# A feature-map attention and a Mish feed-forward in one core: other loads at the start, bias by columns, nine filler products, and a new order of all steps

## The chip, the cores and the metric

The kernel runs on one core of a Trainium2 chip. The metric is the device time of one execution in microseconds (us). A core has five engines that run side by side and wait for each other by semaphores: PE (matrix products), DVE and POOL (vector work), ACT (functions of one operand), SP (here it only issues DMAs). The instructions of one engine run in the order in which they are written.

## The reference

```python
x = A_x                                    # 1 x 2048 x 448, bf16
xn = _layernorm(x)
# A: 16 heads of 28 columns
q, k, v = split(xn @ wqkv)
phi_q = concat(softmax(q @ w_phi), softmax(-q @ w_phi))
phi_k = concat(softmax(k @ w_phi), softmax(-k @ w_phi))
kv = phi_k^T @ v ;  z = sum of phi_k over the rows
o = (phi_q @ kv) / (phi_q @ z + 1e-6)
# B: 448 -> 1792 -> 448
h = xn @ w1 + b1
act = h * tanh(softplus(h))                # Mish
out = x + o @ wo + act @ w2
```

## The kernel before, in words

**Tiles.** The 2048 rows are 16 tiles (t) of 128 rows, handled as 8 pairs (u). A pair is normalised (statistics on DVE, L472 and L473, 1/sqrt on ACT or POOL, the scaling on DVE, ACT or POOL) and transposed to `xnT`: pairs 3 and 1 by PE in two parts (`xT_part`, L530, with an evacuation in `evac`, L565 on ACT or L567 on DVE), the other six by a DMA that transposes (L572, on SP's queue). For the key and query features the kernel first multiplies the weights with `w_phi`: the key weights are transposed on PE (`w_tr`, L612), the query weights come transposed by four DMAs (`load_qT`, L292; `double_qT`, L296, copies a part of them), and `w_mm` (L641) multiplies both with a block-diagonal `Wbd` that POOL fills (`w_bd`, L595).

**Products.** Every value (v), key (k), query (q) and first feed-forward (f) step is a pair of accumulations over 448 rows. 448 is three and a half times 128, so a step has a part F, six products over 128 rows, and a part H, two products over 64 rows each that run beside each other in the two halves of the array. All of them are recorded in `pair_part` (L440), which takes a pair of PSUM banks when the first part of a step is issued and gives it back after the second; there are four such pairs. The step's result leaves the banks by an exponential on ACT (keys L678, queries L740), by a copy on ACT or DVE (values, L565 and L567) or by Mish on ACT (L774). The first F parts of v3, k3, v1 and k1 wait separately for the two halves of `xnT` (`SPLIT`).

**The rest.** The exponentials are normalised by DVE (sum and reciprocal) and POOL (the product, L690 for keys, L755 for queries). The eight `kv` steps (L707) add up keys times values, `kvz` makes the matrix that the `nd` steps (L800) multiply with the query features, which SP's queue has transposed by then (`q_turn`, L763). The outputs are transposed by DMA (L817). Per tile the output is a sum of `g` (L883, 14 products) and `wo` (L899); DVE adds x (L848) and SP stores.

**The order.** `ORDER` is a string with the names of all steps; `run_order` calls them in that order, and each step appends its instructions to its engines' queues. `v3Fd` is part F of the values of pair 3 with DVE as evacuating engine, `lx1s` the load of pair 1's rows on SP, `st7d` the statistics of tile 7 on DVE, `xm7d` the scaling of tile 7 on DVE (`xm7p` on POOL), `xa3a` the first part of the transposition of pair 3 with ACT as evacuating engine, `z10` ten filler products without use (L384), `wtk0b` and `wmk0b` the two halves of the key weights. The string is read together with the waits that `Program.resolve` derives from who writes and reads what.

**What the change touches.** `load_kv_tail` (L286) brings the last 64 rows of key and value weights in one DMA of 896 columns, `load_v_tail` (L289) the value columns a second time into the upper 64 partitions, since H products of the second tile read there; the upper half of the key tail is set to zero by DVE (`p_wz`, L348). `load_b1` (L309) brings the bias as 14 rows of 128, and `bias_T` (L768) turns them by a product on PE and a copy on DVE.

Of the kernel before, what the change touches and what calls it, by code (L numbers as in the profile page):

```python
# [151 lines left out]
ORDER = """  # L152
pm pw lx3s pk pz lkms lkts lvms lvts lpa table pi lx1s lqT0 lx2s st6d rt6a st7d z10 rt7a lqT1 lx4s lqT2 lqT3 xm6d lx0s
pv wtk0b lx6s xm7d xa3a wtk1b bd wmk0b xb3a st3d wmk1a st2d v3Fd st5d rt3p rt2a xm2d v3Ha xm3d lbs k3F st4d xa1a k3H
xb1d v1Fa qd wmq1a rs2p st11d xn2d wmq0a st10d k1F b1 k1H st13d rs5p xn5p v1Ha q1H q3H st9d st12d q1F q3F xt2m q2F k2F
st8d st0d k2H rs4p v2Hd st1d l1m1s xt5m xn4d rs6p rs0p l1m2s xt4m q2H xn6p st15d st14d v2Fd rs7p xt6m k5F xn0p q5F pp
q5H xn7d k5H v4Ha k4H v4Fd qn6p xt7m l1m0s k4F qn4p q6F k6F v5Ha q6H qn7p qn2p k7H xt0m l1ts e7 k6H v5Fd kn3.0 k7F q7F
v6Fa q7H kn1.1 kn4.1 kn1.0 q0H qn13p f1.0H v6Ha q0F kn2.1 f1.0F f0.1F f0.5F v0Fd f0.1H f0.5H f1.2H kn3.1 v0Hd f1.2F
f1.5F f1.4H f1.5H k0H kn7.0 kn6.1 kn2.0 v7Hd kn7.1 ep f1.4F k0F v7Fd qn14p q4F f1.3F q4H kn5.1 e6 f0.2H f1.3H f0.0H
kn0.1 f0.2F f0.0F e2 f0.3F e4 kn6.0 kv7 e14 kn5.0 kn0.0 kv1 kv3 f0.9H f0.3H f0.9F los f1.1F kn4.0 f0.13F f0.10F f0.13H  # L160
f1.1H qn11p qn12p kv5 kv0 kv6 kv2 kv4 f0.12H f0.6H f0.10H f0.6F qn3p kvz qn9p f0.12F qn5p f1.6F e3 qn1p f1.6H qn8p
f0.4H f1.10H f0.7H qn0p f1.10F f0.4F nd7 wob e5 qn15p f0.7F nd4 f1.9F f0.11F f1.12F f0.11H f1.12H f1.8H f1.9H f1.8F
f1.7F f1.13F qn10p l2s f1.13H e15 f1.11H f0.8H f1.7H e9 f0.8F nd2 f1.11F nd6 e8 g5 nd3 nd5 e11 e10 e12 g8 ot3m ot1m
ot2m nd8 g3 g9 nd9 ot4m nd11 g2 wo2F wo3F e13 wo4H e1 wo1H wo2H wo3H wo1F g4 nd10 wo4F nd13 ot5m sto2 nd14 g7 g6 nd15
e0 g13 sto4 sto1 nd0 nd1 wo5F g14 ot7m ot0m g10 nd12 g12 g0 wo7F g1 ot6m wo0H wo7H wo6H wo5H wo6F stt14 sto3 g11 wo0F
sto0 sto5 sto6 g15 stt15
"""
# [7 lines left out]
def _kernel(es, nc, A_x, A_wqkv, A_w_phi, A_wo, B_w1, B_b1, B_w2, out):  # L175
    def sb(name, shape, dtype):
        return es.enter_context(nc.sbuf_tensor(name, shape, dtype))
# [588 lines left out]
    def bias_T():  # L766
        b = take1()
        pe(lambda e: e.transpose(bank16(b)[:, 0:FC], b1_rows[0:FC, :], ident[0:FC, 0:FC]), [("b1r",), ("ident",)],  # L768
           [pb(b)], "b1")
# [275 lines left out]
```

## Time and profile before

| | |
|---|---|
| median of 3 runs | 151.9 us (151.89 to 152.0) |
| the profiled execution | 151.9 us, of which its span is 150.4 us |
| busy time DVE, ACT, POOL | 90.3 us (60%), 71.4 us (47%), 70.4 us (47%) |
| DMA | 16.97 MB in 39480 packets, mean 113 GB/s |
| shares of the chain that ended last | PE 89%, SP's queue 5%, DMA 2%, DVE 1% |

The span runs from the first instruction to the last; 1.5 us of the execution lie outside it. A start in the rows below is counted from the start of the span. The busy time of PE is that of pipelined products whose ends overlap, so how fast PE runs is read from the distance between starts, not from the duration of one.

### The profile page before, as it was taken

The page shows a single profiled execution, that of the slowest core. Times are in us where ns is not written, and L with a number is a line of the kernel's source. Part 1 is how long each engine was busy: PE and PEld are TensorE (multiplying, and loading weights), DVE is VectorE, ACT ScalarE, POOL GpSimd, SP SyncE. Part 2 cuts the span into 40 slices and gives each one's busy share as a digit, 9 for nine tenths or more (in the row PEclk, how much of TensorE's full clock was granted, in tenths as well). Part 3 has the DMA queues.
Part 4 walks back from the last instruction along what each step waited for, and adds up shares of the span by engine and source line. Part 5 has one row for each costly group of instructions (what it writes and reads, how often), then busy time and mean ns, then how long its engine had stood idle before and what let it go on. Part 6 is the DMA issues. An engine that isn't in the chain of part 4 may idle for free.

```text
span 150.4 us, 2592 instructions
## 1 busy us (share of the span) xinstructions
PE 146.1 (97%) x1051; PEld 72.3 (48%) x1051; DVE 90.3 (60%) x180; ACT 71.4 (47%) x85; POOL 70.4 (47%) x77
## 2 busy tenths in 40 slices
PE   7899999999999999999999999999999999999992
PEld 2554444444443535454354445555455555554451
DVE  0997996899999899947986004514049351200641
ACT  3688998989986979546681974000000000000000
POOL 7522799399999999998999100000000000000000
PEclk9999999999999999999999999999999999999999
DMA  5997696796830009401479994530905933030206
GB/s 131 271 234 215 127 251 114 142 226 40 174 70 0 0 0 126 162 0 29 80 145 355 155 197 89 101 65 9 188 3 39 256 86 61 0 65 0 92 0 214
DMA packets 39480, 16.97 MB, mean 113 GB/s; under 512 B 33452, under 2 KB 38700, under 8 KB 39468
## 3 DMA queue, kind: packets, MB, share of 16 engines
q1 hardware_dynamic: 38860, 16.68, 51.6%
q10 hardware_dynamic: 608, 0.12, 0.4%
q8 instruction: 8, 0.13, 0.3%
q14 instruction: 4, 0.03, 0.1%
HBM read 6.97 MB, written 1.84 MB: 59 GB/s over the span
## 4 chain that ended last, share of the span: by engine, by line
PE 89%; SPq 5%; DMA 2%; DVE 1%; issue 0%
PE PS L440 49%; PE PS L883 28%; PE PS L899 7%; PE PS L800 2%; DMA WqT<-in_A_wqkv_dram 2%; SPq L292 2%; PE PS L707 2%; SPq L271 1%; SPq L274 1%; PE PS L641 1%; DVE x_all L848 0%; SPq L286 0%; SPq L289 0%; DVE WqT L296 0%; DVE x_all L869 0%
## 5 line engine op out<-in xcount | busy, mean ns | idle before, releaser
L440 PE MATMUL PS<-xnT,W 128*128 128x512 bf16 (+1 forms) x224 | 45.5, 379 | 0.0
L883 PE MATMUL PS<-W,actT 128*128 128x448 bf16 (+1 forms) x224 | 44.0, 351 | 0.0
L774 ACT ACTIVATE actT<-PS,b1T 128x1024 bf16<-128x1024 f32 x28 | 30.1, 1113 | 13.3 <-PE PS L440 13.1
L883 PEld LDWEIGHTS PS<-W,actT 128*128 128x128 bf16 x224 | 21.4, 98 | 18.8
L440 PEld LDWEIGHTS PS<-xnT,W 128*128 128x128 bf16 (+1 forms) x224 | 17.6, 97 | 24.4 <-issue 5.4
L755 POOL TENSOR_TENSOR EqS<-EqS,rSk 128x896 bf16<-128x896 bf16 x16 | 26.7, 1694 | 3.0 <-DVE rSk L753 3.0
L690 POOL TENSOR_TENSOR actT<-actT,rSk 128x896 bf16<-128x896 bf16 x16 | 26.6, 1693 | 0.0
L848 DVE TENSOR_TENSOR x_all<-PS,x_all 128x448 bf16<-128x448 f32 (+1 forms) x16 | 9.5, 617 | 20.8 <-PE PS L899 14.4
L805 DVE RECIPROCAL rden<-PS 128x16 f32<-128x16 f32 x16 | 4.0, 250 | 24.2 <-PE PS L800 24.2
L751 DVE TENSOR_REDUCE Sk<-EqS 128x32 f32<-128x896 bf16 x16 | 16.7, 1042 | 0.0
L686 DVE TENSOR_REDUCE Sk<-actT 128x32 f32<-128x896 bf16 x16 | 16.5, 1033 | 0.0
L740 ACT ACTIVATE EqS<-PS 128x896 bf16<-128x896 f32 x16 | 13.8, 943 | 2.6 <-PE PS L440 2.6
L678 ACT ACTIVATE actT<-PS 128x896 bf16<-128x896 f32 x16 | 13.7, 941 | 0.2 <-PE PS L440 0.2
L440 PE MATMUL PS<-Wkv,xnT 128*128 128x448 bf16 (+1 forms) x64 | 13.2, 353 | 0.0
L440 PE MATMUL PS<-Wpk,xnT 128*128 128x448 bf16 (+1 forms) x64 | 13.0, 353 | 0.0
L440 PE MATMUL PS<-Wpq,xnT 128*128 128x448 bf16 (+1 forms) x64 | 12.5, 353 | 0.0
L472 DVE BATCH_NORM_STATS2 stats<-x_all 128x6 f32<-128x448 bf16 x16 | 9.7, 608 | 2.6 <-DMA x_all<-in_A_x_dram 2.6
L807 DVE TENSOR_TENSOR xn<-PS,rden 128x448 bf16<-128x448 f32 x16 | 10.0, 625 | 0.6
L440 PEld LDWEIGHTS PS<-Wpq,xnT 128*128 128x128 bf16 (+1 forms) x64 | 5.2, 97 | 6.2 <-issue 1.9
L440 PEld LDWEIGHTS PS<-Wkv,xnT 128*128 128x128 bf16 (+1 forms) x64 | 5.0, 97 | 6.0 <-issue 1.9
L440 PEld LDWEIGHTS PS<-Wpk,xnT 128*128 128x128 bf16 (+1 forms) x64 | 5.3, 97 | 5.2 <-issue 0.6
L567 DVE CAST v_all<-PS 128x896 bf16<-128x896 f32 x5 | 5.4, 1079 | 2.3 <-PE PS L440 2.3
(80 smaller groups left out, 108.7 us busy)
## 6 DMA issues: line engine op xcount, KB each, us to landing
W<-in_B_w_dram SPq DMA_DIRECT2D x1, 1568.0 KB, 9.0
out_dram<-x_all SPq DMA_DIRECT2D x7, 224.0 KB, 2.3
W<-in_B_w_dram SPq DMA_DIRECT2D x3, 448.0 KB, 3.9
x_all<-in_A_x_dram SPq DMA_DIRECT2D x4, 224.0 KB, 3.5
x_all<-in_A_x_dram SPq DMA_DIRECT2D x2, 448.0 KB, 4.2
Wkv<-in_A_wqkv_dram SPq DMA_DIRECT2D x2, 336.0 KB, 4.1
Wo<-in_A_wo_dram SPq DMA_DIRECT2D x2, 336.0 KB, 4.0
W<-in_B_w_dram SPq DMA_DIRECT2D x2, 224.0 KB, 4.7
```

The lines of the kernel that those rows point to most:

```text
L440: ins = e.matmul(o, lhs(c, k), rhs(c, k), start=first and c in (0, 3), stop=not first and c in (2, 3))
L472: op("DVE", lambda e: e.bn_stats(stats[:, t, :], x_all[:, t, :]), r=[("x", t)], w=[("st", t)], tag=f"bn{t}")
L678: op("ACT", lambda e, s=s: e.activation(E_of(u)[:, s, :, :], two(b, D), ACT.Exp, scale=1.0 if s == 0 else -1.0), r=[pb(b), pb(b + 1)], w=[ ...
L686: op("DVE", lambda e: e.tensor_reduce(Sk[u][:, s, :], Eh(), AX.X, ALU.add), r=[("E", u, s)], w=[("Sk", u, s)], tag=f"Sk{u}.{s}")
L690: op("POOL", lambda e: e.tensor_tensor(Eh(), Eh(), ap_on(rSk[u][:, s, 0:1], [[1, 2 * H], [0, DH]]), ALU.mult), r=[("E", u, s), ("rSk", u, ...
L740: op("ACT", lambda e, s=s: e.activation(EqS[:, k:k + 2, :, s * QP:(s + 1) * QP], two(b, D).rearrange("p i (h n) -> p i h n", n=QP), ACT.Ex ...
L751: op("DVE", lambda e: e.tensor_reduce(ap_on(Sk[u][:, i, 0:1], [[4, 2 * G], [1, 4]]), E, AX.X, ALU.add), r=both, w=[("Sk", u, i)], tag=f"Sq ...
L755: op(eng, lambda e: e.tensor_tensor(E, E, ap_on(rSk[u][:, i, 0:1], [[4, 2 * G], [1, 4], [0, DH]]), ALU.mult), r=both + [("rSk", u, i)], w= ...
L774: op("ACT", lambda e: e.activation(actT[:, fc, q * 1024:(q + 1) * 1024], bank(b, 2), ACT.Mish, bias=b1T[:, fc:fc + 1]), r=[("b1T",), pb(b) ...
L807: op("DVE", lambda e: e.tensor_tensor(o_sb[u % NXN][:, i, :].rearrange("p (h d) -> p h d", d=DH), ap_on(bank(b)[:, 0:1], [[NC, H], [1, DH] ...
L883: ins = e.matmul(bank(b)[:, 0:width(t)], actT[:, fc, tok(t)], W2[:, fc, 0:width(t)], start=first and fc == 0, stop=last and fc == FC - 1)
L899: ins = e.matmul(bank(b)[:, 0:n], oT_of(u)[lo:hi, cc * P:(cc + 1) * P], Wo[lo:hi, cc, 0:n], start=first and c in (0, 3), stop=last and c i ...
```

## The change

The key tail is a DMA of its own (448 columns, 64 rows), and the value tail is loaded twice, once for each half of the partitions, so there are three tail loads where there were two. The rows of pair 1 are issued ahead of the value weights. The bias comes as a 128 by 14 array, element by element, and DVE copies it; the product on PE and its bank are gone. There are nine filler products in place of ten. And `ORDER` is another string. These are the parts of the diff beside it, with its first line:

```diff
-pm pw lx3s pk pz lkms lkts lvms lvts lpa table pi lx1s lqT0 lx2s st6d rt6a st7d z10 rt7a lqT1 lx4s lqT2 lqT3 xm6d lx0s
+lx3s pz lpa pw pm lkms table lkts lx1s lvms lvt0s lvt1s st7d pi rt7a bd st6d rt6a z9 wtk0b xm7p xm6d wtk1b lx4s xa3a
...
-    b1_rows = sb("b1_rows", [FC, P], BF16)
+    b1_cols = sb("b1_cols", [P, FC], BF16)
...
-    def load_kv_tail(eng):
-        dma(eng, lambda e: e.dma_start(Wkv[0:64, 3, :], A_wqkv[384:448, D:3 * D]), w=[("Wt", 0)], tag="ldWkt")
-
-    def load_v_tail(eng):
-        dma(eng, lambda e: e.dma_start(Wkv[64:128, 3, D:2 * D], A_wqkv[384:448, 2 * D:3 * D]), w=[("Wt", 1)], tag="ldWvt")
+    def load_k_tail(eng):
+        dma(eng, lambda e: e.dma_start(Wk[0:64, 3, :], A_wqkv[384:448, D:2 * D]), w=[("Wt", 2)], tag="ldWkt")
+
+    def load_v_tail(i, eng):
+        lo, hi = HALF[i]
+        dma(eng, lambda e: e.dma_start(Wv[lo:hi, 3, :], A_wqkv[384:448, 2 * D:3 * D]), w=[("Wt", i)], tag="ldWvt")
...
-            return [(name, 0), ("Wt", 0), ("Wz",) if name == "Wk" else ("Wt", 1)]
+            return [("Wk", 0), ("Wt", 2), ("Wz",)] if name == "Wk" else [("Wv", 0), ("Wt", 0), ("Wt", 1)]
...
-        dma(eng, lambda e: e.dma_start(b1_rows[:], B_b1.rearrange("(c p) -> c p", p=P)), w=[("b1r",)], tag="ldb1")
+        dma(eng, lambda e: e.dma_start(b1_cols[:], B_b1.rearrange("(c p) -> p c", p=P), allow_slow_non_contiguous=True), w=[("b1r",)], tag="ldb1")
...
-        b = take1()
-        pe(lambda e: e.transpose(bank16(b)[:, 0:FC], b1_rows[0:FC, :], ident[0:FC, 0:FC]), [("b1r",), ("ident",)],
-           [pb(b)], "b1")
-        evac("DVE", lambda: b1T[:], lambda: bank16(b)[:, 0:FC], [pb(b)], [("b1T",)], "b1e")
+        op("DVE", lambda e: e.tensor_copy(b1T[:], b1_cols[:]), r=[("b1r",)], w=[("b1T",)], tag="b1e")
...
-    for n in (4, 8, 10, 12, 14, 16, 18, 20):
+    for n in (4, 8, 9, 10, 12, 14, 16, 18, 20):
```

DVE at the start, from the first statistics (tiles 6 and 7) on. `EqS` is here the place of the transposed key weights, `xn3` the normalised rows of pair 3, `Wpk` the key weights multiplied with `w_phi`. Before:

```order
L520 TENSOR_SCALAR xn3<-x_all,mv,rstd 128x448
L567 COPY EqS<-PS 112x512
L520 TENSOR_SCALAR xn3<-x_all,mv,rstd 128x64
L520 TENSOR_SCALAR xn3<-x_all,mv,rstd 128x384
L567 COPY EqS<-PS 112x512
L567 CAST Wpk<-PS 128x448
L472 BN_STATS stats<-x_all 128x6
```

And now, from the same place on:

```order
L568 COPY EqS<-PS 112x512
L506 SCALAR_TENSOR_TENSOR shift<-mv,rstd 128x1
L521 TENSOR_SCALAR xn3<-x_all,mv,rstd 128x448
L568 COPY EqS<-PS 112x512
L473 BN_STATS stats<-x_all 128x6
L474 BN_AGGR mv<-stats 128x2
...
L568 COPY xnT<-PS 128x512
L568 CAST Wpk<-PS 128x448
```

The scaling of tile 7 has left DVE (POOL has it), the copy of the second half of pair 3's `xnT` has come to DVE, and the statistics of tiles 3 and 2 now stand ahead of that copy and of the cast.

PE from the value product of pair 3 to the query weights. `xn1` are the rows of pair 1; a row with x6 and no wait joins six products. Before:

```order
L440 MATMUL PS<-Wkv,xnT 128x448 [waits dma_3,dma_4]
...
L440 MATMUL PS<-Wkv,xnT 128x448 [waits done_ACT]
...
L440 MATMUL PS<-Wpk,xnT 128x448 [waits done_DVE,done_ACT]
...
L530 MATMUL PS<-ident,xn1 128x128 [waits done_DVE]
...
L440 MATMUL PS<-Wpk,xnT 128x448 x2
...
L440 MATMUL PS<-Wkv,xnT 128x448 [waits done_DVE]
...
L641 MATMUL PS<-Wbd,WqT 128x112 [waits done_DVE]
...
L440 MATMUL PS<-Wpk,xnT 128x448 x6
L768 MATMUL PS<-ident,b1_rows 128x14 [waits dma_14,done_ACT]
```

And now:

```order
L441 MATMUL PS<-Wkv,xnT 128x448 [waits dma_5,dma_4,dma_6,done_ACT]
...
L441 MATMUL PS<-Wkv,xnT 128x448 [waits done_DVE]
...
L441 MATMUL PS<-Wpk,xnT 128x448 [waits done_ACT,done_DVE]
...
L531 MATMUL PS<-ident,xn1 128x128 [waits done_DVE]
...
L531 MATMUL PS<-ident,xn1 128x128 [waits done_ACT]
...
L441 MATMUL PS<-Wpk,xnT 128x448 x6
L441 MATMUL PS<-Wpk,xnT 128x448 [waits done_ACT]
...
L642 MATMUL PS<-Wbd,WqT 128x112 [waits done_DVE]
...
L441 MATMUL PS<-Wkv,xnT 128x448 [waits done_ACT]
```

The second half of v3 now waits for DVE, the two transpositions of pair 1 stand between the H and the F part of k3, the query weights come after k1 in place of before it, and the bias product is gone.

SP's queue from its first row to the first transposition of normalised rows (`xnT<-xn1` is pair 5, `xnT<-xn2` pair 2). Before:

```order
L274 DMA Wkv<-in_A_wqkv_dram 128x3x448
L286 DMA Wkv<-in_A_wqkv_dram 64x896
L289 DMA Wkv<-in_A_wqkv_dram 64x448
L271 DMA x_all<-in_A_x_dram 128x896
L292 DMA_TRANSPOSE WqT<-in_A_wqkv_dram 128x448
...
L271 DMA x_all<-in_A_x_dram 128x1792
L292 DMA_TRANSPOSE WqT<-in_A_wqkv_dram 128x448 x2
...
L309 DMA b1_rows<-in_B_b1_dram 14x128
L572 DMA_TRANSPOSE xnT<-xn2 128x7x128 [waits dma_12,dma_13,done_DVE]
```

And now:

```order
L286 DMA Wkv<-in_A_wqkv_dram 64x448
L271 DMA x_all<-in_A_x_dram 128x896
L274 DMA Wkv<-in_A_wqkv_dram 128x3x448
L290 DMA Wkv<-in_A_wqkv_dram 64x448 x2
L271 DMA x_all<-in_A_x_dram 128x1792
L293 DMA_TRANSPOSE WqT<-in_A_wqkv_dram 128x448 x4
...
L573 DMA_TRANSPOSE xnT<-xn1 128x7x128 [waits dma_12,dma_13,done_POOL]
```

The four transposed loads of query weights now follow each other without rows of x between them, pair 2's rows have moved from ahead of three of them to behind all four, the bias has left this stretch, and the first transposition of normalised rows belongs to pair 5 and waits for POOL.

The new string also moves later steps. Before, q4 was the last of the v, k and q steps, between f1.4 and f1.3; now q0 is the last, around the F part of f1.9, with exponentials on ACT among the Mish steps. The eight `kv` steps stood in two groups of three and five and now stand in one. Counting the steps on PE, the H parts formed 18 groups and form 17.

More of the change, by code (lines that the diff above doesn't have):

```diff
@@ L152 @@
 ORDER = """
-pm pw lx3s pk pz lkms lkts lvms lvts lpa table pi lx1s lqT0 lx2s st6d rt6a st7d z10 rt7a lqT1 lx4s lqT2 lqT3 xm6d lx0s
[L154 to L166, printed above, removed]
+lx3s pz lpa pw pm lkms table lkts lx1s lvms lvt0s lvt1s st7d pi rt7a bd st6d rt6a z9 wtk0b xm7p xm6d wtk1b lx4s xa3a
+st3d wmk0a st2d xb3d wmk1b rt2a lqT0 lqT3 rt3p v3Fd xm3a v3Ha xm2d lqT1 k3H st11d xa1a lqT2 lx0s st10d lx6s rs5p xb1a
@@ new lines @@
+k3F lx2s k1F st9d qd xn5p st8d xt5m rs4a wmq1a wmq0d v1Fd st13d k1H xn4p v1Ha st14d ep q1H st15d q3H pv st5d q1F q3F
+rs7p v5Fd st4d l1m1s xt4m st12d k5F l1m2s st1d q5F rs6t xn7d pp v5Ha k5H q5H v4Hd st0d rs2p xn2p xt7m rs0p xt2m kn1.0
+lbs kn3.1 xn0d v4Fd q4F k4F q4H pk k4H v7Hd v7Fa kn3.0 xn6d k2F q7F kn5.0 kn4.1 l1ts b1 k2H v2Ha q7H k7H v2Fd k7F q2F
+xt6m k6F v6Ha q2H kn2.1 qn8p xt0m qn7p k6H k0H kn7.1 l1m0s v6Fd k0F q6F f1.2F los q6H f1.2H f0.5H v0Ha f0.5F v0Fa
+kn4.0 kn0.0 e7 f0.3F f0.1F kn1.1 f0.4F kn7.0 f1.3H f0.4H f0.3H f0.1H kn5.1 f1.3F f0.2F f0.0F kn2.0 l2s f1.5F f0.2H
@@ new lines @@
+f1.5H kn0.1 kn6.0 f0.0H kv1 kv2 kv3 kn6.1 kv0 qn3p kv4 kv7 qn6p kv5 kv6 f0.7H e3 f0.8H qn4p f0.9H f0.7F qn15p qn5p
+f0.9F f0.8F f1.0F kvz f1.10H f1.0H e6 f0.12H f1.8H f1.10F nd3 f1.8F qn11p f0.12F f1.11F e5 e4 f0.10F f1.7H f0.10H
+f1.11H f0.11H qn2p f1.7F nd6 nd7 f0.11F f1.6F wob qn12p f1.4H e8 e2 f1.12H e15 f0.6H f1.6H f0.6F qn13p ot3m f1.4F nd2
+f1.12F nd5 f0.13F f1.1H ot1m f0.13H f1.9H q0H f1.9F nd15 qn9p nd4 q0F g3 qn1p g2 ot2m nd8 e9 e12 f1.1F qn14p g5 wo3H
+e11 qn0p qn10p e14 f1.13H e10 wo2H wo1H f1.13F wo1F wo2F nd9 wo3F nd14 e1 e0 g10 g6 nd10 nd11 ot4m sto1 g7 g4 nd0 e13
@@ L167 @@
+nd12 g8 nd1 nd13 g13 ot5m ot0m g9 ot6m wo5F ot7m g0 wo6H wo0H wo4H wo5H g11 wo4F g14 wo7F wo7H g12 g1 sto2 wo6F sto4
+wo0F sto6 sto3 g15 sto0 sto5 stt14 stt15
 """
@@ L238, in _kernel @@
     oT_home = [(Wkv, 0, ["Wk", "Wv"]), (Wkv, 14 * P, []), (WqT, 0, ["Wq"]), (Wp[1], 0, ["Wp1"])]
-    home_rows = {"Wk": [("Wk", 0), ("Wt", 0), ("Wt", 1), ("Wz",)], "Wv": [("Wv", 0)], "Wq": [("WqT", g) for g in range(G)] + [("WqTd",)],
+    home_rows = {"Wk": [("Wk", 0), ("Wz",)] + [("Wt", i) for i in range(3)], "Wv": [("Wv", 0)], "Wq": [("WqT", g) for g in range(G)] + [("WqTd",)],
                  "Wp1": [("Wp", 1, h, c) for h in range(2) for c in range(2)]}
@@ L969, in _kernel @@
     add("table", table)
-    add("bd", w_bd)
     for eng, c in (("SP", "s"), ("ACT", "a")):
@@ L975, in _kernel @@
             add(f"l{n}m{c}", load_main, eng, "W" + n, t, A_wqkv[:, (i + 1) * D:(i + 2) * D])
-        add(f"lkt{c}", load_kv_tail, eng)
-        add(f"lvt{c}", load_v_tail, eng)
+        add(f"lkt{c}", load_k_tail, eng)
+        for i in range(2):
+            add(f"lvt{i}{c}", load_v_tail, i, eng)
         for i in range(3):
@@ L984, in _kernel @@
         add(f"lqT{g}", load_qT, g, "SP")
+    add("bd", w_bd)
     add("b1", bias_T)
```

## The prediction

> **What bounds the kernel now.** The page's first part gives PE 97% of the span, so I went on to PE's waits, then to the chain of waits, then to the timeline of the first 26 us. PE's waits are two:
>
> ```profile
> PE PS L384 <- PEq L1030: 0.8, 1, 0.8
> PE PS L530 <- DVE xn L520: 0.2, 1, 0.2
> ```
>
> The chain, in order of time (start, length, what):
>
> ```profile
> 3.48 0.58 SPq L271
> ...
> 7.81 1.12 SPq L292
> ...
> 8.97 3.54 DMA WqT<-in_A_wqkv_dram
> ...
> 12.54 0.24 DVE WqT L296
> ...
> 12.83 0.96 PE PS L641 x16
> ...
> 14.98 0.16 PE PS L768
> 15.15 43.46 PE PS L440 x242
> ...
> 76.76 0.22 PE PS L800 x8
> 76.98 1.30 PE PS L440 x6
> ...
> 91.46 2.65 PE PS L883 x14
> ...
> 147.08 0.02 issue
> ```
>
> Until 15 us SP's issues, a DMA, DVE and gaps have a part in it; from 15.15 to 147.08 there is PE alone. The pace of PE is read from the last rows: 14 products of 448 columns in 2.65, 0.189 each; six of 512 columns in 1.30, 0.216; eight of an `nd` in 0.22. What lies behind q1H, which begins at 15.47 (row below), is 406 units of 448 columns (76.8; an H pair is one unit), 196 of 512 (42.4), 128 products of `kv` and 128 of `nd` at 0.027 (6.9), and a last tile of 14 products (2.3): 128.4, and the trace needs 131.5 until its last columns. The 3 us left are the changes between F and H:
>
> ```profile
> 23.55 1.59 PE L440 MATMUL PS<-Wpq,xnT 128*128 128x448 bf16 x8
> 24.98 0.35 PE L440 MATMUL PS<-Wpk,xnT 64*128 64x448 bf16 x2
> ...
> 25.36 0.35 PE L440 MATMUL PS<-Wpk,xnT 64*128 64x448 bf16 x2
> 25.64 0.55 PE L440 MATMUL PS<-Wkv,xnT 128*128 128x448 bf16 x2
> ```
>
> H pairs follow each other at 0.19, but six F products and a pair take 1.43 (23.55 to 24.98) where 7 units are 1.32, and the last pair takes 0.28: about 0.1 for each change of mode, 32 of them behind q1H, 3.2 us. So the interior has no wait to remove. A change can gain ahead of 15.47 and by fewer changes of mode, and can lose everywhere.
>
> **The change part by part.** Ahead of q1H both programs have the same products to do (v3, k3, v1, k1, both weight products, four transpositions), so the question is when q1H begins. The rows I build on:
>
> ```profile
> 4.88 0.62 PE L612 MATMUL PS<-ident,Wkv 128*112 128x128 bf16 x8
> ...
> 5.26 0.41 DVE L520 TENSOR_SCALAR xn<-x_all,mv,rstd 128x448 bf16<-128x448 bf16 x1
> ...
> 5.59 0.41 DVE L567 COPY EqS<-PS 112x512 bf16<-112x512 bf16 x1
> ...
> 7.08 0.62 DVE L567 CAST Wpk<-PS 128x448 bf16<-128x448 f32 x1
> ...
> 7.40 0.55 PE L641 MATMUL PS<-Wbd,EqS 112*128 112x112 bf16 x8
> ...
> 7.79 1.60 PE L440 MATMUL PS<-Wkv,xnT 128*128 128x448 bf16 x8
> ...
> 8.49 0.59 DVE L472 BATCH_NORM_STATS2 stats<-x_all 128x6 f32<-128x448 bf16 x1
> ...
> 9.22 0.59 DVE L472 BATCH_NORM_STATS2 stats<-x_all 128x6 f32<-128x448 bf16 x1
> ...
> 9.31 1.31 PE L440 MATMUL PS<-Wpk,xnT 128*128 128x448 bf16 x6
> ...
> 11.37 1.31 PE L440 MATMUL PS<-Wkv,xnT 128*128 128x448 bf16 x6
> ...
> 13.63 1.30 PE L440 MATMUL PS<-Wpk,xnT 128*128 128x448 bf16 x6
> ...
> 15.47 4.05 PE L440 MATMUL PS<-Wpq,xnT 64*128 64x448 bf16 x22
> ```
>
> Two groups of POOL (shape, count | busy, mean ns | idle before):
>
> ```profile
> L547 POOL TENSOR_SCALAR xn<-x_all,rstd,shift 128x384 bf16<-128x384 bf16 x3 | 2.1, 701 | 0.0
> ...
> L547 POOL TENSOR_SCALAR xn<-x_all,rstd,shift 128x64 bf16<-128x64 bf16 x3 | 1.2, 397 | 0.0
> ```
>
> And of the DMA issues (size, us from issue to landing; the last row is of the transpositions to `xnT`):
>
> ```profile
> Wkv<-in_A_wqkv_dram SPq DMA_DIRECT2D x1, 56.0 KB, 4.3
> ...
> W<-in_B_w_dram SPq DMA_DIRECT2D x1, 1568.0 KB, 9.0
> ...
> Wraw<-in_A_w_phi_dram ACTq DMA_DIRECT2D x1, 24.5 KB, 3.1
> ...
> DMA to landing us min/median/max: 2.9/3.2/4.5
> ```
>
> *v3.* Places on SP's queue I turn into times with the chain's rows, 0.4 to 0.6 an issue and 1.15 a transposing one, from 0.8 on. The key weights are still second, so PE's first transposition stays at 4.88. DVE now copies its result (5.59 to 6.0) ahead of the scaling of tile 6, which ends at 6.5 (0.8 later than before); the second copy ends at 6.9. Then stand the statistics of tiles 3 and 2, 0.73 each by the two starts, to 8.35 (their rows are issued at 2.25 and land by 6.55 even at the 4.3 of the third tail, in time), and only then the copy of v3's second half, to 8.75. POOL scales tile 7 from 6.2 to 7.3 (0.40 + 0.70); PE's transposition and the second key product (0.3 + 0.4) follow, and v3 begins at 8.05 in place of 7.79. Its first half ends at 8.6, its second runs from 8.75 to 9.3. Before, v3 made room at 9.31: nothing won or lost. The value weights are two places later; their last tail is issued at 4.05 and lands at 7.7 if I go by bytes in flight, at 8.35 by the 4.3 of its row, which would cost up to 0.2; I take no wait. [...] A key tail of half the bytes lands earlier and hastens nothing, since PE then waits for tile 6.
>
> *k3 to q1H.* The H parts of v3 and k3 form one group and end at 9.8. Then PE waits for tile 2, scaled by DVE behind the cast (0.55, to 9.3) and a shift, at 9.75, and for tile 3 (ACT, about 10.15): transposed by 10.45, some 0.2 of it idle. k3F takes 1.15 to 11.6, k1F to 12.75. The fourth transposed weight load is issued at about 8.85 (before 8.97, the chain's row) since pair 2's rows now come behind it; 3.54 later it is there, doubled by 12.75: the query weights run from 12.8 to 13.6 without the 0.3 that PE lost before (v1F's six products from 11.37 end at 12.5, the next row of the chain begins at 12.83). v1F ends at 14.75, then k1H, v1H, and q1H at 15.23. Before, 14.77 to 15.08 went to the bias, whose rows PE waited for (0.2) and whose product it made (0.1). Sum: 15.47 - 15.23 = 0.24 won. The bounds are the neighbours' spread: 0.2 on DVE's chain either way, and up to 0.3 worse if the fourth weight load takes 3.85 as the third tail's 4.3 makes possible.
>
> Rows of ACT and POOL that the next parts need:
>
> ```profile
> 21.08 1.80 ACT L678 ACTIVATE actT<-PS 128x896 bf16<-128x896 f32 x2
> ...
> 22.67 1.83 ACT L740 ACTIVATE EqS<-PS 128x896 bf16<-128x896 f32 x2
> ...
> 40.37 1.28 ACT L774 ACT_TABLE_LOAD   x1
> ...
> 44.44 9.97 POOL L690 TENSOR_TENSOR actT<-actT,rSk 128x896 bf16<-128x896 bf16 x6
> ```
>
> *Costs at nothing.* The tenth filler ran while PE had to wait for the keys until 4.88; without that cover it would be 0.2. The bias as 1792 single elements is bounded by the 3.1 of 448 small runs and the 9.0 of 1792 long ones; it is issued at about 25 and needed at 41. POOL's mask for `kvz` moves among the key normalisations: 18 products at 1.66 and 1.7 for the mask, from about 25 (its scalings at the two groups above, added up), end at 56.6 (six take 9.97); the last `kv` stands at 58.5, so 1.9 cover it, and what was missing PE would lose. q0 at the end makes ACT load its table twice more, 1.28 each; its banks are free at 93, PE wants them at 95.7.
>
> *Modes.* 31 changes behind q1H in place of 32: 0.1 won.
>
> *First transposed rows.* v5 is the first step that reads a pair transposed by DMA. It stands at 18.0 (two H, then q1F and q3F at 1.15). POOL scales pair 5 (three parts, 1.8) from 12.95, when DVE has made its shift behind the doubling, to 14.8; SP also waits for the last rows of x; it issues at 14.95, and at the median of 3.2 the rows are there at 18.15. I put 0.1 lost.
>
> The sum: -0.24 - 0.1 + 0.1 = -0.24. The tail, 3.3 us from 147.1, has the same last tile and stays. The profiled execution took 151.9 with a span of 150.4, its time is the median of the runs; so 151.7. About 0.3 us, 0.2%, is what a measurement can tell from no change: 151.6 to 152.2 is "same".
>
> **The rivals.**
>
> *Late transposition (slower).* The same v5, with the 4.5 that one of the six took behind a weight load: here pair 2's rows are in flight ahead of it. Rows at 19.45, 1.45 lost in place of 0.1: 153.0. It cancels the gain from a landing of 3.5 and is measurably slower from 3.8. For it: no slack at all; against: the first transposition of before was issued at the same time.
>
> *Cold PE.* The ten fillers (start, length) show the clock:
>
> ```profile
> 0.84 3.91 PE L384 MATMUL PS<-const-bfloat16-1.0 128*128 128x512 bf16 x10 [0.84 <-PEq L1030]
> ```
>
> Ten products of 512 columns would be 2.16 at the later pace of 0.216; they took 3.91, so PE ran at half pace for about 2 x 1.75 = 3.5 us, until some 0.4 before their end. If it falls back in the emptier stretch from 4.4 to 8.05, 3.65 us with only transpositions and small products (before 4.75 to 7.79, 3.0 us, without harm), the next 3.5 us, as long as the first slow stretch, hold 2.3 us of products at double cost: 154.0. [...]
>
> *ACT falls behind.* A pair of exponentials takes 1.6 (21.08 to 22.67). From 15.1 ACT has exk1, ve1, exq1, exq3, four small ones for pair 6 (1.0), ve5 and exk5 before k4F may take k5's banks: 24.3, and k4F stands at 24.5. If the pairs did not overlap and took the row's 1.80, four of them would be 0.8 longer and k4F 0.6 late: 152.3. Against it: the rows do overlap.
>
> *No gain.* A fourth weight load of 3.8 delays the query weights by 0.25: 151.9, the waits have only moved.
>
> *More gain.* If the waits at 8.6, 9.8, 10.1 and 18.0 all vanish, 0.4 more: 151.3.
>
> **How the numbers follow.** My forecast 0.44, with its own range 151.4 to 152.0 (more than half of it, 0.24, under 151.6); more gain 0.18; no gain 0.13; ACT 0.06; late transposition 0.12; cold PE 0.07. Faster 0.24 + 0.18 = 0.42; same 0.20 + 0.13 = 0.33; slower 0.06 + 0.12 + 0.07 = 0.25. The range goes from 151.1, below "more gain", to 152.6, which takes in ACT and a part of the late transposition; cold PE, the rest of the late transposition and stray ends stay out, under 0.2.
>
> **What would show it.** q1H (the first product with `Wpq`) at 15.2; v3 beginning near 8.05 with a gap of 0.1 in its middle; PE idle by 0.2 ahead of the transpositions of pair 1; no wait between k1F, the query weights and v1F; v5 at 18.0 to 18.2. Wrong it would be with a row of PE waiting anywhere behind 19, with products 0.38 apart behind 8, or with q1H at 15.5 and later.

## The result, and the profile after

| | median of its runs | range, number of runs | ratio to the kernel before, 95% interval |
|---|---|---|---|
| before | 152.03 us | 151.89 to 152.56, 6 | |
| after | 153.63 us | 153.52 to 154.01, 6 | 1.0102 [1.0082, 1.0121] |

The change makes the kernel 1.6 us slower; the forecast was 151.7, and its range ended at 152.6. The profiled execution of the changed kernel took 154.01 with a span of 152.3, that of the kernel before 151.9 with 150.4: 2.1 us between the two, since it is the longest of its six runs. PE's waits, in the changed kernel (what waited, what for, us in total, times, longest):

```profile
PE PS L441 <- DVE v_all L568: 1.6, 1, 1.6
PE PS L613 <- DMA Wkv<-in_A_wqkv_dram: 0.4, 1, 0.4
PE PS L531 <- DVE xn L521: 0.4, 1, 0.4
```

The first row has no counterpart before: a product waits 1.6 us for DVE's copy of a value pair to `v_all`. The chain of the changed kernel shows where (start, length, what):

```profile
1.25 3.85 DMA Wkv<-in_A_wqkv_dram
...
25.49 3.64 DVE xn L553 x3
29.13 1.01 DVE v_all L568
30.19 28.02 PE PS L441 x152
58.21 3.27 PE PS L708 x128
...
147.00 2.29 PE PS L881 x14
149.32 0.56 DVE x_all L846
```

Before, the chain was PE alone from 15.15. Now it is PE alone only from 30.19. The product that starts there is F of k2 (`k2F`): it needs the two banks that v4 holds, v4 leaves them by DVE's copy (29.13), and the copy stands in DVE's queue behind the scaling of pair 0 (`xn0d`), which takes 3.64 us. From 30.19 to 149.3 PE waits for nothing. More of the difference lies ahead of q1H, the first product with `Wpq`. PE's timeline of the changed kernel (start, length, what):

```profile
0.84 4.00 PE L385 MATMUL PS<-const-bfloat16-1.0 128*128 128x512 bf16 x9 [0.84 <-PEq L1029]
5.23 1.57 PE L613 MATMUL PS<-ident,Wkv 128*112 128x128 bf16 x16 [0.40 <-DMA Wkv<-in_A_wqkv_dram]
...
8.73 1.62 PE L441 MATMUL PS<-Wkv,xnT 128*128 128x448 bf16 x8
...
13.49 0.95 PE L642 MATMUL PS<-Wbd,WqT 112*128 112x112 bf16 x16
...
15.96 2.92 PE L441 MATMUL PS<-Wpq,xnT 64*128 64x448 bf16 x16
```

The transposition of the key weights begins at 5.23 (before 4.88), v3 at 8.73 (before 7.79), q1H at 15.96 (before 15.47). So the span is longer by 1.62 of waiting and 0.49 of a later q1H, and shorter by 0.2 in what lies behind q1H otherwise: 1.9, which is 152.3 less 150.4. The rest of the 2.1 between the two executions lies outside the span, where the kernel before spends 1.5 (151.9 less 150.4) and the changed one 1.7 (154.01 less 152.3).

**The scaling that takes 3.64.** DVE's rows in the changed kernel:

```profile
20.98 0.86 DVE L553 TENSOR_SCALAR xn<-x_all,mv,rstd 128x448 bf16<-128x448 bf16 x3
...
25.49 3.64 DVE L553 TENSOR_SCALAR xn<-x_all,mv,rstd 128x448 bf16<-128x448 bf16 x3
29.06 1.08 DVE L568 CAST v_all<-PS 128x896 bf16<-128x896 f32 x1
...
31.43 2.19 DVE L553 TENSOR_SCALAR xn<-x_all,mv,rstd 128x448 bf16<-128x448 bf16 x3
```

And POOL's of the same time:

```profile
25.42 3.38 POOL L691 TENSOR_TENSOR actT<-actT,rSk 128x896 bf16<-128x896 bf16 x2
...
31.60 1.70 POOL L691 TENSOR_TENSOR actT<-actT,rSk 128x896 bf16<-128x896 bf16 x1 [0.83 <-DVE rSk L689]
```

The same three scalings take 0.86 at 20.98, when POOL has only a step of 0.73 on 2 columns (20.81), and 3.64 at 25.49, beside two products of the key normalisation; pair 6's take 2.19 beside one. The end of the scalings (29.13) lies 0.33 behind the end of POOL's products (28.80). One by one they take 1.76, 1.80 and 0.37 here: the first two end just behind a product each (27.25 and 28.97, the products at 27.12 and 28.80), though the second has only 64 columns. DVE's copy out of PSUM takes its usual 1.08.

### The profile page after: what moved, and what is told of

Read it like the earlier page. It is cut to its first block, busy times and chain, and to the rows that moved or that the text cites. A ratio compares the mean times of both kernels' runs of the same rounds, so it can differ in the third digit from the quotient of the medians.

```text
span 152.3 us, 2597 instructions
## 1 busy us (share of the span) xinstructions
PE 146.2 (96%) x1049; PEld 72.3 (47%) x1049; DVE 92.1 (61%) x178; ACT 74.7 (49%) x93; POOL 69.8 (46%) x75
## 3 DMA queue, kind: packets, MB, share of 16 engines
HBM read 6.97 MB, written 1.84 MB: 58 GB/s over the span
## 4 chain that ended last, share of the span: by engine, by line
PE 82%; DVE 9%; DMA 3%; POOL 2%; ACT 1%; issue 1%; SPq 0%
PE PS L441 40%; PE PS L881 28%; PE PS L897 7%; DVE xn L553 3%; DVE stats L473 3%; DMA Wkv<-in_A_wqkv_dram 3%; PE PS L798 2%; PE PS L708 2%; POOL xn L548 1%; DVE mv L474 1%; PE PS L642 1%; DVE Wpq L568 1%; POOL xn L517 1%; PE PS L613 1%; ACT xn L513 1%
## 5 line engine op out<-in xcount | busy, mean ns | idle before, releaser
L553 DVE TENSOR_SCALAR xn<-x_all,mv,rstd 128x448 bf16<-128x448 bf16 (+2 forms) x9 | 6.7, 816 | 0.1
```

What stands on the lines that cost most here:

```text
L553: op("DVE", lambda e, t=t, lo=lo, hi=hi, at=at: e.tensor_scalar(X[:, at:at + hi - lo], x_all[:, t, lo:hi], mv[:, t, 0:1], rstd[:, t:t + 1] ...
```

## The experiments

Theory A was that a product of POOL holds DVE's scaling off; its rivals were the head of the kernel (B) and a DVE queue that is too full at that place (C). All ratios are to the kernel before.

**1. Pair 0's scaling back on POOL.**

```diff
-lbs kn3.1 xn0d v4Fd
+lbs kn3.1 xn0p v4Fd
```

> The changed kernel with pair 0's scaling given back to POOL (behind its two key products); DVE keeps only its shift. Theory A, the meeting: DVE's scaling of pair 0 took 3.64 us in place of 0.86 because it ran beside POOL's two key products, and the copy of v4 behind it kept k2F 1.78 us. Then the wait ahead of k2F is gone and 1.3 to 1.8 come back: 151.8 to 152.3. Theory B, the head: the time is lost ahead of q1H (15.96 in place of 15.47) and grows behind it: 153.2 to 153.7, a wait of like size at another place. Theory C, DVE's queue: the copy of v4 simply stands behind too much work; taking 0.9 us of scaling at its usual length away brings 0.7 to 0.9: 152.7 to 152.9.

Measured: 152.2 us, ratio 1.001 [0.9997, 1.0022]. The wait ahead of k2F is gone and 1.4 us have come back, as A has it (B and C had at most 0.9). DVE's rows of this run:

```profile
25.13 1.65 DVE L541 SCALAR_TENSOR_TENSOR shift<-mv,rstd 128x2 f32<-128x2 f32 x1
26.70 1.08 DVE L568 CAST v_all<-PS 128x896 bf16<-128x896 f32 x1
...
29.08 0.79 DVE L553 TENSOR_SCALAR xn<-x_all,mv,rstd 128x448 bf16<-128x448 bf16 x3
```

and POOL's:

```profile
25.07 3.36 POOL L691 TENSOR_TENSOR actT<-actT,rSk 128x896 bf16<-128x896 bf16 x2
28.41 2.00 POOL L548 TENSOR_SCALAR xn<-x_all,rstd,shift 128x448 bf16<-128x448 bf16 x3
```

The first row is the clearest of all. The shift is an instruction on 2 columns that takes 0.13 to 0.15 elsewhere; here it begins 0.06 behind a product and ends 1.65 later, when that product (1.68) ends. What held it cannot be its size. Pair 6's scaling runs beside scalings of POOL instead of a product, and it is those that are longer (2.00; 1.74 at 22.38 of the same run).

**2. POOL's mask steps ahead of its products.** Only POOL's order changes; DVE's rows are the same, one by one.

```diff
-xt2m kn1.0
+xt2m pk kn1.0
...
-q4F k4F q4H pk k4H
+q4F k4F q4H k4H
```

> The changed kernel with the order of POOL alone changed: its five steps of the mask for kvz (some 2.0 us) ahead of its key products of pairs 1 and 3 in place of behind them. DVE's queue is the same, row by row. Theory A, the meeting: DVE's scaling of pair 0 runs beside mask steps, not beside two-input products, and takes 0.9 to 1.4; the copy of v4 comes in time; 151.8 to 152.4. If mask steps stretch it too, 2 us or more and 152.8 to 153.6. Theory C, DVE's queue: nothing changes for DVE, 153.5 to 153.7. Theory B, the head: 153.5 to 153.7.

Measured: 152.98 us, 1.0059 [1.0037, 1.0081]. DVE's rows:

```profile
25.05 0.89 DVE L553 TENSOR_SCALAR xn<-x_all,mv,rstd 128x448 bf16<-128x448 bf16 x3 [0.15 <-POOL rstd L482]
25.86 1.08 DVE L568 CAST v_all<-PS 128x896 bf16<-128x896 f32 x1
...
28.24 4.18 DVE L553 TENSOR_SCALAR xn<-x_all,mv,rstd 128x448 bf16<-128x448 bf16 x3
```

With an unchanged queue of its own, DVE scales pair 0 beside mask steps in 0.89 in place of 3.64, and the wait ahead of k2F is gone: C falls, and B, which had at least 153.5. But the products now run later, three in a row, as POOL's row shows:

```profile
27.27 5.04 POOL L691 TENSOR_TENSOR actT<-actT,rSk 128x896 bf16<-128x896 bf16 x3
```

They meet the scaling of pair 6, which takes 4.18. Its transposition is issued late, and PE waits for it:

```profile
35.58 1.29 PE L441 MATMUL PS<-Wpk,xnT 128*128 128x448 bf16 x6 [0.54 <-DMA xnT<-xn]
```

So the time missed the 151.8 to 152.4 that A gave by 0.6: the mechanism was right, and a second place of it was not reckoned with.

**3. The copy of v4 ahead of the scaling.**

```diff
-kn3.1 xn0d v4Fd q4F k4F
+kn3.1 v4Fd xn0d q4F k4F
```

> The changed kernel with DVE's copy of v4 one step earlier, ahead of the scaling of pair 0; POOL's order is the same. Theory A, the meeting: the scaling still meets POOL's products and takes 2 to 3.7 us, but nobody waits for it: the wait ahead of k2F is gone, 151.8 to 152.3. Theory B, the head: 153.4 to 153.7. Theory C, DVE's queue: 152.7 to 152.9, as the other run that takes the scaling out of v4's way.

Measured: 153.17 us, 1.0067 [1.0044, 1.009], outside what A gave. The scaling still meets the products (2.91) and delays nobody, but everything behind it on DVE is late, pair 6's scaling too:

```profile
26.05 2.91 DVE L553 TENSOR_SCALAR xn<-x_all,mv,rstd 128x448 bf16<-128x448 bf16 x3
...
30.26 2.46 DVE L553 TENSOR_SCALAR xn<-x_all,mv,rstd 128x448 bf16<-128x448 bf16 x3
```

and the same k6F waits, by 0.81 (0.98 by the starts). In the changed kernel this wait could not be seen, since PE was already 1.6 late.

**4. Both scalings out of the way, by DVE's order alone.**

```diff
-kn3.1 xn0d v4Fd q4F k4F
+kn3.1 v4Fd xn0d q4F k4F
...
-v7Fa kn3.0 xn6d k2F
+v7Fa xn6d kn3.0 k2F
```

> The changed kernel with the copy of v4 ahead of the scaling of pair 0, and the scaling of pair 6 ahead of the sums of the keys of pair 3 (only DVE's order; POOL's and PE's are the same). By the meeting theory pair 6 is now scaled beside mask steps in 0.9 to 1.2, its transposed rows are there in time, and both waits of PE between 28 and 36 us are gone: 151.9 to 152.4. If only DVE's load counts, the second wait stays, 153.0 to 153.3.

Measured: 152.2 us, 1.0004 [0.9986, 1.0022]. Neither wait is left. DVE's six scalings of pairs 0 and 6 in one row, the last three beside mask steps:

```profile
25.84 3.75 DVE L553 TENSOR_SCALAR xn<-x_all,mv,rstd 128x448 bf16<-128x448 bf16 x6
```

They end at 29.59, where in the changed kernel pair 6's alone end at 33.62. In the profiled execution (152.65) PE waited at another place, for pair 4's transposed rows:

```profile
22.79 1.42 PE L441 MATMUL PS<-Wkv,xnT 64*128 64x448 bf16 x7 [0.31 <-DMA xnT<-xn]
```

**5. The same, and a weight chunk issued behind that transposition.**

```diff
-st4d l1m1s xt4m
+st4d xt4m l1m1s
```

> The changed kernel with both scalings out of the products' way (152.2 by its own run, where PE waited 0.56 at 22.1 for the transposed rows of pair 4) and the first chunk of the first feed-forward weights issued behind that transposition in place of ahead of it. If that chunk delays the rows: landed by 21.4, no wait, 151.7 to 152.0. If the wait was of that execution alone: 152.0 to 152.3.

Measured: 152.08 us, 0.9989 [0.997, 1.0008]; no wait of PE behind 11 us. (The wait that the expectation puts at 0.56 is 0.31 in the row of run 4.) The time does not differ measurably from run 4, so that the chunk caused the wait at 22.8 isn't shown. What is shown: without the two meetings the changed kernel's time is that of the kernel before.

**6. POOL's products halved.**

```diff
-        op("POOL", lambda e: e.tensor_tensor(Eh(), Eh(), ap_on(rSk[u][:, s, 0:1], [[1, 2 * H], [0, DH]]), ALU.mult),
+        for i in range(2):
+            op("POOL", lambda e, i=i: e.tensor_tensor(Eh()[:, i * H:(i + 1) * H, :], Eh()[:, i * H:(i + 1) * H, :],
...
```

> The changed kernel with each of POOL's sixteen key products cut into two of half the size. If a product holds DVE off for its whole length and each scaling of DVE gets through between two of them, the three scalings of pair 0 wait for halves of 0.85 to 0.9: 2.1 to 2.9 us in place of 3.64, k2F waits 0.4 to 1.1, 152.6 to 153.2 if POOL's longer time harms nothing else. If the two engines share the memory in proportion, the scalings stay at 3.4 to 3.8 and the time at 153.5 to 153.8.

Measured: 154.54 us, 1.0158 [1.0135, 1.0181], slower than either theory said. DVE's scaling, POOL's half products, PE's wait ahead of k2F and the end of the `kv` steps on PE:

```profile
25.50 2.90 DVE L553 TENSOR_SCALAR xn<-x_all,mv,rstd 128x448 bf16<-128x448 bf16 x3
```

```profile
25.43 3.88 POOL L692 TENSOR_TENSOR actT<-actT,rSk 128x448 bf16<-128x448 bf16 x4
```

```profile
PE PS L441 <- DVE v_all L568: 0.9, 1, 0.9
```

```profile
61.61 0.58 PE L710 MATMUL PS<-actT,v_all 128*60 128x112 bf16 x16 [1.31 <-POOL actT L692]
```

The scalings take 2.90 in place of 3.64, and the wait ahead of k2F falls from 1.6 to 0.9: DVE gets one scaling through per piece of POOL's work (2.90 / 3 = 0.97 a scaling, 3.88 / 4 = 0.97 a piece), and the piece is now shorter. That speaks for a hold that lasts one instruction and against a share of bandwidth. The time is lost at the other end: four halves take 3.88 where two wholes took 3.38, POOL is late with the last keys, and `kv` waits 1.31.

**7. Ten fillers.**

```diff
-st6d rt6a z9 wtk0b
+st6d rt6a z10 wtk0b
```

> The changed kernel with ten filler products in place of nine. Theory F, the tenth filler: with nine, PE is not busy long enough before the keys' transposition, its pace doubles only at 6.25 us and the first steps are late; with ten the pace doubles before 5.3 and q1H comes at 15.4 to 15.6: 153.0 to 153.3. Theory G: the moment at which the pace doubles does not hang on the tenth filler; it may come anywhere from 4 to 6.3 us, q1H at 15.9 to 16.2, 153.5 to 153.9.

Measured: 154.01 us, 1.0121 [1.0099, 1.0143], above both ranges; against the changed kernel the intervals overlap. q1H, at 15.74, lies between the two theories, but the pace does not double before 5.3, as F had it. PE's first rows here:

```profile
0.84 4.43 PE L385 MATMUL PS<-const-bfloat16-1.0 128*128 128x512 bf16 x10 [0.84 <-PEq L1029]
5.17 1.35 PE L613 MATMUL PS<-ident,Wkv 128*112 128x128 bf16 x16
```

and those of run 1, with nine:

```profile
0.84 3.41 PE L385 MATMUL PS<-const-bfloat16-1.0 128*128 128x512 bf16 x9 [0.84 <-PEq L1029]
5.31 1.07 PE L613 MATMUL PS<-ident,Wkv 128*112 128x128 bf16 x16 [1.06 <-DMA Wkv<-in_A_wqkv_dram]
```

The fillers of the changed kernel start 0.43 apart, half the pace of the 0.216 that a product of 512 columns takes later; its key transpositions start 0.107 apart until about 6.2 and 0.056 apart behind it. At full pace the 16 transpositions take 1.07. With ten fillers they took 1.35, so the pace doubled about 2 x 0.28 behind 5.17, at 5.7; in run 1, with nine fillers, which took 3.41 where nine at half pace take 4.00, it doubled at about 4.25 - 0.59 = 3.7; in the changed kernel (1.57) at about 5.23 + 2 x 0.50 = 6.2. Over these three executions the moment varies by 2.5 us, and the tenth filler doesn't set it. What sets the moment the runs don't show.

**8. The value weights ahead of the second rows** (with the edit of run 1).

```diff
-lx1s lvms lvt0s
+lvms lx1s lvt0s
```

> The changed kernel with pair 0's scaling on POOL (152.2 by its own run) and, besides, the main value weights issued ahead of the second rows, as in the kernel before. Theory D, the neighbour: the key weights land at 5.1 in place of 4.75 because rows of x, in pieces of 1792 bytes in place of 896, run behind them; then keys land at 4.7 to 4.8, q1H comes at 15.2 to 15.3 and the time is 151.8 to 152.0. Theory T: the later landing has another cause (the key tail's half size, the number of loads): keys at 5.05 to 5.15, q1H at 15.5 to 15.9, 152.1 to 152.3.

Measured: 152.36 us, 1.0015 [0.9999, 1.003]. The key transposition starts at 5.17, near the 5.23 of the changed kernel, and q1H comes at 15.82, both as T has it. So D is not borne out; since the start varies by 0.3 in the kernel before alone (run 9), one profile does not settle it.

**9. Two more executions of the kernel before.** No edit.

> The kernel before, unchanged, looked at once more, for what varies ahead of q1H. So far its one profile has the main key weights landed at 4.74 and PE's pace doubled at 4.2, the changed kernel's family 5.0 to 5.2 and a doubling anywhere from 3.6 to 6.2. Theory V: both moments vary from execution to execution in this kernel too; then keys at 4.7 to 5.7, a doubling at another time, q1H at 15.4 to 16.2, and total time less q1H again 136.4. Theory S: the landing at 4.74 belongs to this kernel: 4.7 to 4.8 again.

> The kernel before once more, as a third look at what varies ahead of q1H. Theory V: keys at 4.7 to 5.7 and another moment of the doubling of pace. Theory S: keys at 4.7 to 4.8.

The first execution took 152.76 us. PE's rows:

```profile
5.19 0.62 PE L612 MATMUL PS<-ident,Wkv 128*112 128x128 bf16 x8
...
15.49 2.92 PE L440 MATMUL PS<-Wpq,xnT 64*128 64x448 bf16 x16
19.09 1.10 PE L440 MATMUL PS<-Wpq,xnT 128*128 128x448 bf16 x5 [0.68 <-DMA xnT<-xn]
```

The second took 151.62; its rows:

```profile
5.06 0.66 PE L612 MATMUL PS<-ident,Wkv 128*112 128x128 bf16 x8
...
15.21 4.05 PE L440 MATMUL PS<-Wpq,xnT 64*128 64x448 bf16 x22
```

Theory V holds for the keys: their transposition, which began at 4.88 in the first profile, begins at 5.19 and 5.06 here. A q1H at 15.21 is earlier than the 15.4 that V gave. And the first of the two has the late transposition that the forecast kept as a rival for the changed kernel: 0.68 of waiting at 18 us, in the kernel before.

**10. The load part alone, in the kernel before.**

```diff
-lkts lvms lvts lpa
+lkts lvms lvt0s lvt1s lpa
...
```

with `load_k_tail` and `load_v_tail` of the change.

> The kernel before with the load part alone: the key tail comes alone, the value tail twice, all other loads in the old order (each behind them one issue later). Theory K, the smaller tail: with 56 KB behind them in place of 112 the main key weights land at 5.0 to 5.2 in place of 4.75, and PE is 0.2 to 0.3 later: 152.2 to 152.4. Theory S2: the tail has no part in it: keys at 4.7 to 4.8, 151.9 to 152.1.

Measured: 153.91 us, 1.0109 [1.0074, 1.0145], slower than both theories said. The keys start at 4.89 in this execution, so the smaller tail does not delay them here. Two other waits appear on PE:

```profile
13.65 0.96 PE L642 MATMUL PS<-Wbd,WqT 112*128 112x112 bf16 x16 [0.74 <-DVE WqT L297]
...
20.06 1.11 PE L441 MATMUL PS<-Wpq,xnT 128*128 128x448 bf16 x5 [0.89 <-DMA xnT<-xn]
```

The query weights and the first transposed rows, both loaded on SP's queue behind the added tail, are late. The kernel before can have both waits too (0.21 and 0.68 in the first execution of run 9). The new order has neither, although it has the third tail as well. Of the 1.9 us that this run loses, 0.3 lie outside the span (see below).

**11. The bias alone, in the kernel before, early.**

```diff
-        b = take1()
-        pe(lambda e: e.transpose(bank16(b)[:, 0:FC], b1_rows[0:FC, :], ident[0:FC, 0:FC]), [("b1r",), ("ident",)],
...
+        take1()
+        op("DVE", lambda e: e.tensor_copy(b1T[:], b1_cols[:]), r=[("b1r",)], w=[("b1T",)], tag="b1e")
```

> The kernel before with one part of the change: the bias loaded by columns and turned into f32 by a copy on DVE, at the places where its load and its step stood (the bank that its product took is still counted, so all others keep theirs). Step (bias) of the prediction: PE loses no 0.3 us between k1F and k1H; 151.6 to 151.8 where the kernel before has 152.0. Rival: 1792 single elements, issued at 9 us among weight loads and rows, delay these; the query weights come late and the gain is eaten: 152.0 to 152.5.

Measured: 152.28 us, 1.0015 [1.0001, 1.0029]: no gain in time, as the rival has it. The load is issued at 11.35 and lands 5.0 us later; the copy holds DVE's queue until then:

```profile
16.41 0.17 DVE L768 CAST b1T<-b_cols 128x14 f32<-128x14 bf16 x1 [1.24 <-DMA b_cols<-in_B_b_dram]
```

No later wait of PE follows from it in this profile; the keys began at 5.83 in this execution, 0.95 later than in the first profile of before, and q1H only 0.43 later (15.90).

**12. The bias alone, late.** Issued at 30 us, copied behind the sums of the keys of pair 3.

```diff
-v3Ha xm3d lbs k3F
+v3Ha xm3d k3F
...
-xt0m l1ts e7 k6H v5Fd kn3.0 k7F
+xt0m l1ts lbs e7 k6H v5Fd kn3.0 b1 k7F
```

> The kernel before with the bias by columns as in the run of the bias alone, but issued behind the first weights' tails at about 25 us, as in the changed kernel, and copied behind the sums of the keys of pair 3. Theory L: issued early its 1792 elements landed late and kept DVE 1.2 us, or delayed other loads; late it costs nothing and PE saves the 0.3 of the bias product: 151.6 to 151.8. Theory N: the saved 0.3 is not seen in the time because the moment of q1H is set by loads and the doubling of pace: 152.0 to 152.3.

Measured: 152.72 us, 1.003 [1.0005, 1.0055], above both ranges. A product waits for an exponential:

```profile
PE PS L440 <- ACT actT L678: 0.7, 1, 0.7
```

The step `b1` still takes a bank's turn, and since it now stands elsewhere the later steps get other banks; that the wait comes of this is argued from the order.

**13. The bias alone, late, with the turn of the banks kept.** Beside the edit of run 12:

```diff
-k1F k1H st13d rs5p
+k1F turn k1H st13d rs5p
...
-kn4.1 kn1.0 q0H
+kn4.1 b1 kn1.0 q0H
```

where `turn` counts the bank that the product took and does nothing.

> The kernel before with the bias by columns, issued at 30 us and copied behind the sums of the keys of pairs 1 and 4, and this time with the turn of the banks kept as it was (in the run of the late bias it had shifted, and PE waited 0.85 at 33.6 for an exponential). Theory L: PE saves the 0.3 of the bias between k1F and k1H and pays nothing elsewhere: 151.6 to 151.8. Theory N: what is saved there is not seen, since the query weights or the first transposed rows are what sets q1H and v5: 151.9 to 152.1.

Measured: 151.74 us (151.49 to 152.06, 12 runs), 0.9972 [0.9954, 0.9991]: quicker than both kernels. PE's first transposition of the keys, F of k1 with its H behind it, and q1H:

```profile
5.32 0.90 PE L612 MATMUL PS<-ident,Wkv 128*112 128x128 bf16 x8
...
13.86 1.60 PE L440 MATMUL PS<-Wpk,xnT 128*128 128x448 bf16 x8
...
15.49 4.06 PE L440 MATMUL PS<-Wpq,xnT 64*128 64x448 bf16 x22
```

The keys are 0.44 later than in the first profile of before, with q1H at nearly the same time. No wait of PE is left. The copy also stands later than in run 12, so which of the two edits removed the wait there isn't told apart.

## Why the prediction was wrong

**The step that failed** is the part "Costs at nothing". It lists what the change moves beside other work, and the scaling of pair 0, which leaves POOL for DVE (`xn0p` becomes `xn0d`) and now stands directly ahead of the copy of v4, is not in it; POOL's key products, which now begin at 25, are in it for their own end alone and are not laid beside DVE. So the scaling went in at its usual 0.86 and with no wait behind it. It took 3.64 and PE lost 1.62 (runs 1 to 3 and 6 show that it is this). Two of the three signs of being wrong that the prediction named came: a wait of PE behind 19, and q1H later than 15.5. The trace of the kernel before had the price in it. POOL's row, and DVE's two, of that kernel:

```profile
24.39 1.87 POOL L547 TENSOR_SCALAR xn<-x_all,rstd,shift 128x448 bf16<-128x448 bf16 x3
```

```profile
19.92 0.86 DVE L552 TENSOR_SCALAR xn<-x_all,mv,rstd 128x448 bf16<-128x448 bf16 x3
...
24.45 1.36 DVE L552 TENSOR_SCALAR xn<-x_all,mv,rstd 128x448 bf16<-128x448 bf16 x3 [0.68 <-POOL rstd L481]
```

The same three scalings take half as long again when they start 0.06 behind work of POOL. There a scaling of 0.4 to 0.7 held DVE; the products that the change puts in its place are 1.7 each. Up to three products may hold three scalings, up to 5 us by this estimate, so a bound of 0.86 to some 5 would have stood in the range. Beside a product of POOL the three scalings go from 0.86 to 3.64 (changed kernel) and the shift from 0.13 to 1.65 (run 1), while DVE's copy out of PSUM (1.08 at 26.70) and its sums (1.07 at 27.70) keep their length beside one in run 1. A short step of POOL did not hold DVE: the one of 0.73 on 2 columns began 0.17 ahead of the scaling at 20.98, which kept its 0.86.

**v3, k3, and q1H at 15.23.** Measured 15.96. The distance from the first transposition of the keys to q1H, which is what was worked out, was forecast as 15.23 - 4.88 = 10.35. It was 10.28 in runs 1 and 4 (15.59 - 5.31, 15.43 - 5.15) and 10.73 in the changed kernel, where PE's pace doubled only at 6.2. The waits are there, for tiles 6, 7 and 3 (0.39, 0.17 and 0.17), and the query weights follow k1F without one. The second value tail landed at about 8.0 (4.03 + 4.0), between the 7.7 and the 8.35, and no product waited for it. What failed was the beginning: 4.88 was a property of one execution. It is 5.06 and 5.19 in the two other executions of the kernel before, 5.32 to 5.83 in the three runs of the bias with the old loads, and 5.15 to 5.31 in the nine profiles of the changed kernel and its variants; whether the new loads have a part in it stays open. Nor was the 15.47 of before a fixed mark: q1H comes at 15.21, 15.47 and 15.49 in its three profiles, and at 15.43 to 15.96 in those nine. The same distance is 10.59, 10.30 and 10.15 in the three profiles of the kernel before, so by distance too the new head gains nothing over two of them. The 0.24 was not there, and with the pace doubling late the head costs up to 0.5.

**The bias.** The 0.3 that the forecast gave the old bias is too much. From the start of k1F to q1H PE takes 1.84, 1.73 and 1.85 in the three profiles of the kernel before, and 1.63 in runs 11 to 13, without the product: 0.1 to 0.2. In time run 13 gains 0.28% [0.09%, 0.46%], 0.4 us with 0.1 to 0.7 as its bounds; the later load and copy moved in it as well.

**Outside the span.** The sum took as fixed the 1.5 us that an execution spends outside its span, without a reason. Time less span is 1.39 to 1.52 in every execution measured of the kernel before and of runs 11 to 13, and 1.70 to 1.84 in every one of the changed kernel, of runs 1 to 8 and of run 10. Of the change, run 10 has only the loads of the tails, so it is these that cost the 0.3; by what path the traces don't show, since they end with the span. Of the 1.6 us between the medians of the two kernels, 0.3 are of this kind. This is a second term put at nothing, and it explains why runs 4 and 5, without the meetings, end level with the kernel before: their spans, 150.4 and 150.3 in the median, are shorter than the 150.5 and 150.7 of the kernel before measured beside them, and the 0.3 outside takes that back.

**The other terms.** The tenth filler: at nothing, right (run 7). The bias landed in 5.0 us, between the bounds of 3.1 and 9.0, and far ahead of its use. The mask among POOL's products: no wait, but the reasoning was wrong. I had POOL's last key product end at 56.6 and the last `kv` at 58.5, with POOL busy from 25 on; it waits 3.4 us for DVE's reciprocals in between, and PE itself is late. The profile has, on POOL and then on PE:

```profile
52.50 8.32 POOL L691 TENSOR_TENSOR actT<-actT,rSk 128x896 bf16<-128x896 bf16 x5
```

```profile
58.14 3.34 PE L708 MATMUL PS<-actT,v_all 128*60 128x112 bf16 x128
```

POOL ends at 60.82, and the last 16 of 128 products begin near 61.0: of 1.9 us of cover some 0.2 was left. Run 1 shows it, where pair 0's scaling adds 2.0 to POOL and `kv` waits 0.17, and run 6 (1.31). q0 at the end costs no wait, right. The changes of mode: from q1H to the end, less the wait, it is 152.3 - 15.96 - 1.62 = 134.7 against 150.4 - 15.47 = 134.9, so some 0.2 is won behind q1H. The 0.1 of the forecast is not the reason: counted by the products in the traces, there are 31 changes behind q1H in both kernels, and the group of H parts that is saved (v3 with k3) lies ahead of it. What wins the 0.2 stays open.

**First transposed rows.** v5 stands at 18.71 with no wait, so the 0.1 was not lost. The rival "late transposition" did not happen here; it did in an execution of the kernel before (0.68) and in run 10 (0.89). "Cold PE": no run shows PE falling back to half pace in an emptier stretch, which this rival supposed. In run 1 its fillers end at 4.25 and v3 begins at 8.37, with only transpositions and small products in those 4.1 us, and v3 runs at full pace (its 8 products in 1.61, before 1.60). In the changed kernel PE left the half pace late, at the start, which cost some 0.45 (10.73 less 10.28) in that execution. "ACT falls behind" did not happen.

## What to carry to other kernels

Before moving an operation such as this scaling from POOL to DVE, or a long POOL operation to another time, lay the two engines' timelines over each other: here a DVE scaling that began while a product of 1.70 on POOL ran lasted until that product ended (1.76 and 1.80 for the first two of pair 0; the third, with no product left, took 0.37), and the copy of v4 behind them in DVE's queue paid too, with 1.62 of PE. Beside short steps of POOL it did not (0.89 beside mask steps, run 2). When such a meeting is removed, look for the next one before counting the gain; here the second lay 6 us further on and hid behind the first. And a start time from one profile is one execution: what is forecast from it is a distance, not a moment. Last, compare time less span too: here a third tail load went with 0.3 us outside the span (run 10), where no row shows it.

## What the runs showed of the hardware that was not expected

- An instruction of DVE on 128 x 2 elements took 1.65 us in place of 0.13 because a product of POOL had begun 0.06 earlier.
- The moment at which PE's pace doubles lay between 3.7 us (run 1) and about 6.6 (run 12: the eight key transpositions from 5.49 took 1.07, the eight from 6.64 took 0.61), for the same first filler at 0.84; in the changed kernel a late one cost up to 0.5 us ahead of q1H.
- The load of 1792 single elements (3.5 KB) took 5.0 us from issue to landing in the changed kernel and in run 11, and 5.8 in run 12, where it was issued at 30.34.
- With three tail loads in place of two, the time outside the span is 1.70 to 1.84 us in place of 1.39 to 1.52, in every execution (run 10 has nothing else of the change).
